# Router logits with tokens on partitions, and the full expert groups ahead of two rests

## The chip, the cores and the metric

The kernel runs on one core of a Trainium2 chip. The metric is device microseconds of one execution; lower is better. Before the change the median of three runs is 1096.84 us (1096.45 to 1098.13).

## What is computed

Three stages follow one another, all in float32.

```python
scores = where(causal, -1e9, q @ k.T / sqrt(D) + decay)      # 4 x 8 heads, 576 tokens, D = 64
x = softmax(scores) @ v                                       # reshaped to 2304 tokens x 512
h = x @ w_in;  x = (h * sigmoid(1.702 * h)) @ w_out           # 512 -> 2048 -> 512
noisy = x @ w_gate + log1p(exp(x @ w_noise)) * noise          # 8 experts
top2, weights = two largest of noisy, softmax over the two
out[t] += weight * (relu(x[t] @ w1[e]) @ w2[e])               # for each chosen expert e, 512 -> 1024 -> 512
```

## The kernel before

The program's order is made by a planner (class Planner) while it is built: the work is written as generators, each yields an engine, an estimated duration and a function that emits the instructions, and the planner picks by start time and priority. What it emits is then fixed: every engine, and the DMA queue on SP, works through its own list in order.

Products run on TensorE in pieces: each float32 operand is split into a rounded part (hi, type fp32r) and a remainder (lo), and a product is hi x hi, hi x lo and lo x hi. ScalarE makes hi, VectorE (sometimes POOL) makes lo.

Stages in time: attention by pairs of heads with the first quarter of the dense layer filling in (0 to some 240 us); the dense layer in chunks of 256 tokens and four quarters of its hidden dimension (to some 624 us); the experts (to the end). The last quarter of each chunk (step, line 1316) is followed by that chunk's routing (route, line 1165), nine times in all.

Routing of a chunk: the 256 rows of 512 values (pay) are transposed on TensorE, 4 matmuls for each half of 128 tokens (tr, line 1179), and split into yh and yl. The logits (line 1195) then have the gate weights as the stationary operand, and the tokens run past it:

```python
for kk in range(KD):
    nc.tensor.matmul(lg, wgs[:, kk], yh[:, kk], start=(kk == 0), stop=False)
    nc.tensor.matmul(lg, wgs[:, kk], yl[:, kk], start=False, stop=(kk == KD - 1))
```

Here wgs holds 32 columns, 16 rounded gate and noise weights and their 16 remainders, so lg is 32 partitions by 256 tokens. ScalarE copies it (line 1203), VectorE subtracts (1204), and two more matmuls with the selection matrix sel2 add the two halves and turn the result over (fold, line 1209), so that tokens lie on partitions; VectorE copies that into lz (1215). A chain of some 25 small VectorE instructions follows: noise, two largest, shares, and a place for each token in its expert's table. Four indirect DMAs on POOL (line 1286) scatter the rows into that table in HBM.

Experts: every expert has room for 640 table rows, five blocks of 128. A group (line 1395) is some blocks of one expert: it loads its rows, transposes and splits them, runs the first product (line 1539), relu and split (1522, 1523), the second product (1592), scales the rows and adds them into the output with an indirect DMA (1579). Groups run one after another in the order of the list:

```python
groups = [(e, 0, NBE) for e in EE] + [(e, NBE if e in EE else 0, NB) for e in range(E)]
```

With NEE = 2, NBE = 2 and NB = 5 that is: blocks 0 and 1 of experts 0 and 1 (the early groups, which start before all chunks are routed), then blocks 2 to 4 of experts 0 and 1, then all five blocks of experts 2 to 7. Each group fetches its expert's weights, 4 MB in pieces of 256 KB (wprep, line 357, loads on SP at line 374), however many blocks it has. The late groups wait until the last chunk's rows are scattered. Within a group all blocks are split before its first product is planned.

An expert below PEX (2) is called whole: its rows are loaded block by block (line 1426) and transposed by TensorE (1467). The others are loaded in strided pieces, eight loads and one small one for a group (1429, 1434), and transposed in 32x32 squares by VectorE (1473).

Of the kernel before, what the change touches and what calls it, by code (L numbers as in the profile page):

```python
# [8 lines left out]
F32 = mybir.dt.float32  # L9
FR = mybir.dt.float32r  # L10
# [4 lines left out]
OP = mybir.AluOpType  # L15
AX = mybir.AxisListType
# [1 line left out]
DRAM = bass.MemoryType.DRAM  # L18

TINY = 2.0 ** -15  # L20
PEX = 2
CAP = 640
EARLY = 256
NEE = 2
# [170 lines left out]
def act(n, sbuf=False, extra=0):  # L195
    return (n + (112 if sbuf else 61)) / 1200 + 0.093 * extra


def dve(n):
    return (n + 64) / 960  # L200
# [10 lines left out]
def mm(n, count=1):  # L211
    return count * max(0.109, 0.0024 + n * 0.0004506)
# [12 lines left out]
def tile_attn_mlp_moe(ctx, tc, q, k, v, f, w_in, w_out, gates, noise, w1, w2, out):  # L225
# [3 lines left out]
    nc = tc.nc  # L229
# [5 lines left out]
    E, FE = w2.shape[0], w2.shape[1]  # L235
    NP = B * H // 2
    PPB = H // 2
    KD = DM // 128
    CH = 256
# [27 lines left out]
    banks, dbanks = Tokens(range(2 * ND, 8)), Tokens(range(ND))  # L267
# [4 lines left out]
    def bank(i, name):  # L272
        return bplace[i].tile([128, 512], F32, name=name, tag=f"bank{i}")
# [4 lines left out]
    def c_(shape, name, dt=F32):  # L278
        return const.tile(shape, dt, name=name)

    identf = c_([128, 128], "identf")
# [10 lines left out]
    tokid = c_([128, NTL], "tokid")  # L292
    nzs = c_([128, NTL, E], "nzs")
    wgs = c_([128, KD, 32], "wgs", FR)
    sel2 = c_([64, 16], "sel2", FR)
    self_ = c_([64, 16], "self")
    cumc = c_([128, E], "cumc", BF)
    thr = c_([128, NOV], "thr")
    tiny = c_([1, 1], "tiny")
# [514 lines left out]
    def setup(one, init):  # L814
# [19 lines left out]
        def later():  # L834
            yield ("DMA", 0.1, lambda: nc.sync.dma_start(wgf, gates))
            yield ("DMA", 0.2, lambda: nc.sync.dma_start(nzs, noise))

            def rest():
                nc.vector.tensor_reduce(self_, identf[0:64, 0:64].rearrange("p (a c) -> p c a", c=16), axis=AX.X, op=OP.add)
                nc.vector.tensor_copy(sel2, self_)  # L840
                nc.vector.tensor_copy(wgs[:, :, 0:16], wgf)
                nc.vector.tensor_tensor(wgs[:, :, 16:32], wgf, wgs[:, :, 0:16].bitcast(F32), op=OP.subtract)
            yield ("DVE", 0.6, rest)

            def prest():
                nc.gpsimd.memset(cumc, 0.0)
                nc.gpsimd.memset(floor8, 0.0)
                nc.gpsimd.memset(floor8[:, 0:NEE], float(EARLY))
                nc.gpsimd.iota(iota8, pattern=[[1, E]], base=0, channel_multiplier=0, **io)
                nc.gpsimd.iota(ebase, pattern=[[RS, E]], base=0, channel_multiplier=0, **io)  # L850
                nc.gpsimd.iota(block, pattern=[[128, CAP // 128]], base=0, channel_multiplier=0, **io)
                nc.gpsimd.iota(thr, pattern=[[128, NOV]], base=CAP, channel_multiplier=0, **io)
                nc.gpsimd.iota(tokid, pattern=[[128, NTL]], base=0, channel_multiplier=1, **io)
                nc.gpsimd.memset(padr[:, 0:ROW - 1], 0.0)
                nc.gpsimd.iota(padr[:, ROW - 1:ROW], pattern=[[0, 1]], base=NT, channel_multiplier=1, **io)
            yield ("POOL", 1.5, prest)
            yield ("set", pad_ok)
# [234 lines left out]
    rt = lctx.enter_context(tc.tile_pool(name="route", bufs=2))  # L1092
# [13 lines left out]
    rest = [c for c in range(NCH) if c not in early_c]  # L1106
# [55 lines left out]
    def V(fn, us=0.08):  # L1162
        return ("DVE", us, fn)

    def route(pos, c, pay, evs, rti):
        tt, ts, stt = nc.vector.tensor_tensor, nc.vector.tensor_scalar, nc.vector.scalar_tensor_tensor
# [4 lines left out]
        a, b = yield from stages(2)  # L1171
        yh, yl = [stage(i, [128, KD, CH], FR, f"yt{x}") for i, x in ((a, "h"), (b, "l"))]
        ends = [event(), event()]
# [13 lines left out]
            yield ("set", ends[t])  # L1187
        for t in range(2):
            yield ("go", tr(t))
        for z in ends:  # L1190
            yield z
        bi = yield banks
        lg = bank(bi, "lg")[0:32, 0:CH]

        def logits():
            for kk in range(KD):
                nc.tensor.matmul(lg, wgs[:, kk], yh[:, kk], start=(kk == 0), stop=False)
                nc.tensor.matmul(lg, wgs[:, kk], yl[:, kk], start=False, stop=(kk == KD - 1))
        yield ("PE", mm(CH, 8), logits)
        yield (stok, a)  # L1200
        yield (stok, b)
        lgs = rt.tile([64, CH], FR, name="lgs", bufs=1)
        yield ("ACT", act(CH), lambda: nc.scalar.copy(lgs[0:32], lg))
        yield ("DVE", dve(CH), lambda: tt(lgs[32:64], lg, lgs[0:32].bitcast(F32), op=OP.subtract))
        yield (banks, bi)
        bi = yield banks
        l2 = bank(bi, "l2")[:, 0:32].rearrange("p (t e) -> p t e", t=2)

        def fold():
            for t in range(2):  # L1210
                nc.tensor.matmul(l2[:, t], lgs[:, t * 128:(t + 1) * 128], sel2, start=True, stop=True)
        yield ("PE", 0.2, fold)
        T = lambda n, sh, d=F32: rt.tile([128] + sh, d, name=n)
        lz = T("lz", [2, 16])
        yield V(lambda: nc.vector.tensor_copy(lz, l2), 0.1)
        yield (banks, bi)
        z = lz[:, :, E:2 * E]
        az, u, d, s2 = [T(n, [2, E]) for n in ("az", "u", "d", "s2")]
# [153 lines left out]
    NB = CAP // 128  # L1372
    NBE = EARLY // 128
    EE = list(range(NEE))
    groups = [(e, 0, NBE) for e in EE] + [(e, NBE if e in EE else 0, NB) for e in range(E)]
    W2 = {}
    for gi_, (e, b0, b1) in enumerate(groups):
        for j in range(FB):
# [372 lines left out]
```

## Time and profile before

| | us |
|---|---|
| median of 3 runs | 1096.84 |
| the profiled execution's own time | 1092.42 |
| its span, first to last instruction | 1090.6 |
| TensorE busy in the span | 1066.9 |

In the profile PE is TensorE's matmuls, PEld its weight loads (which overlap with them), DVE is VectorE, ACT ScalarE, POOL GpSimd, and SP the engine whose queue issues most DMAs. L1592 is line 1592 of the kernel. A merged line of the timeline has a count (x4), and its time goes from the first start to the last end. Matmuls are pipelined: one of 512 columns is shown with 0.39 us, but the next starts 0.23 us behind it, so distances between starts tell what a matmul costs. "<-" in brackets names what ended an engine's idle time.

### The profile page before, as it was taken

The numbers are of one execution on the slowest core, as the hardware profiler recorded it, in microseconds if no ns is written. First come the engines' busy times: TensorE is split into PE (matmuls) and PEld (weight loads), VectorE is DVE, ScalarE is ACT, GpSimd is POOL, SyncE is SP. The second block draws the span as 40 slices with busy tenths as digits, with TensorE's granted clock in tenths as the row PEclk, the third lists the DMA queues.
The fourth block names the chain that finished last, engine by engine and source line by source line (L and its number), as shares of the span: only waits on it lengthen the run. The fifth ranks groups of instructions, "written<-read, shape, count | busy, mean of one in ns | idle before, by whom it ended". The sixth has DMA issues, their size and how long they took to land.

```text
span 1090.6 us, 18989 instructions
## 1 busy us (share of the span) xinstructions
PE 1066.9 (98%) x6876; PEld 950.3 (87%) x6876; DVE 704.2 (65%) x1795; ACT 517.7 (47%) x1240; POOL 233.8 (21%) x274
## 2 busy tenths in 40 slices
PE   8999999999999999999999999999999999999996
PEld 7777788899999898999888887998999999999996
DVE  8889979866697468447888886576353535353321
ACT  7887888854554244224333444455342424242321
POOL 4246544200000000000234331132030303030302
PEclk9999999999999999999999999999999999999998
DMA  8888798657679903000122468988555554344413
GB/s 251 272 243 241 212 254 249 179 183 171 251 172 354 356 20 107 11 1 10 41 78 79 156 200 246 223 197 200 144 116 136 108 144 89 115 86 118 95 33 52
DMA packets 106552, 168.84 MB, mean 155 GB/s; under 512 B 15248, under 2 KB 47760, under 8 KB 106448
## 3 DMA queue, kind: packets, MB, share of 16 engines
q1 hardware_dynamic: 97808, 147.52, 46.0%
q0 software_dynamic: 8640, 20.00, 9.1%
q8 instruction: 56, 0.92, 0.4%
q14 instruction: 48, 0.39, 0.1%
HBM read 118.16 MB, written 49.32 MB: 154 GB/s over the span
## 4 chain that ended last, share of the span: by engine, by line
PE 83%; DVE 7%; DMA 3%; issue 3%; ACT 2%; POOL 1%; SPq 0%; POOLq 0%; DVEq 0%; ACTq 0%
PE h L1539 19%; PE ye L1592 19%; PE h L972 18%; PE y L992 17%; PE O L760 3%; PE PT L715 2%; PE S L626 2%; DVE e L601 1%; DMA rv<-in_v 1%; ACT e L607 1%; DMA rk<-in_k 1%; PE tr L1181 1%; DVE pt24l L473 1%; DMA out<-yt,eids 1%; DMA wraw<-in_w 1%
## 5 line engine op out<-in xcount | busy, mean ns | idle before, releaser
L1523 DVE SCALAR_TENSOR_TENSOR hl<-h,hh 128x256 fp32r<-128x256 f32 (+1 forms) x110 | 54.5, 499 | 172.4 <-ACT hh L1522 172.0
L1522 ACT ACTIVATE hh<-h 128x256 fp32r<-128x256 f32 (+1 forms) x110 | 48.9, 446 | 205.5 <-PE h L1539 205.4
L1579 POOL DMA_INDIRECT out<-yt,ids x36 | 61.8, 1717 | 296.9 <-ACT yt L1574 289.6
L992 PE MATMUL y<-wbh,gh 128*128 128x512 f32 x288 | 114.1, 396 | 0.0
L992 PE MATMUL y<-wbh,gl 128*128 128x512 f32 x288 | 112.6, 391 | 0.0
L992 PE MATMUL y<-wbl,gh 128*128 128x512 f32 x288 | 112.4, 390 | 0.0
L944 ACT ACTIVATE t<-h 128x256 f32<-128x256 f32 x144 | 55.2, 385 | 118.1 <-PE h L972 101.4
L1592 PE MATMUL ye<-wbh,hl 128*128 128x512 f32 x283 | 110.8, 392 | 0.0
L1592 PE MATMUL ye<-wbh,hh 128*128 128x512 f32 x283 | 110.7, 391 | 0.0
L1592 PE MATMUL ye<-wbl,hh 128*128 128x512 f32 x283 | 110.3, 390 | 0.0
L607 ACT ACTIVATE e<-e,m 128x128 f32<-128x128 f32 (+2 forms) x144 | 83.3, 581 | 24.7 <-DVE m L601 24.4
L1539 PE MATMUL h<-xtl,wah 128*128 128x256 f32 (+1 forms) x448 | 86.7, 312 | 0.0
L1539 PE MATMUL h<-xth,wah 128*128 128x256 f32 (+1 forms) x448 | 85.6, 312 | 0.0
L1539 PE MATMUL h<-xth,wal 128*128 128x256 f32 (+1 forms) x448 | 85.3, 312 | 0.0
L945 DVE SCALAR_TENSOR_TENSOR t<-t,h 128x256 f32<-128x256 f32 x144 | 59.9, 417 | 38.0 <-ACT t L944 35.2
L947 ACT CAST gh<-t 128x256 fp32r<-128x256 f32 x126 | 51.0, 406 | 56.1 <-DVE t L945 55.7
L1539 PEld LDWEIGHTS h<-xth,wah 128*128 128x128 f32 x448 | 74.3, 188 | 3.8 <-ACT wah L409 0.2
L354 DVE TENSOR_TENSOR gl<-t,gh 128x256 fp32r<-128x256 f32 x127 | 53.3, 422 | 29.6 <-ACT gh L947 28.3
L1539 PEld LDWEIGHTS h<-xtl,wah 128*128 128x128 f32 x448 | 71.5, 188 | 0.7
L1539 PEld LDWEIGHTS h<-xth,wal 128*128 128x128 f32 x448 | 71.3, 188 | 0.0
L354 DVE TENSOR_TENSOR wal<-wraw,wah 128x512 fp32r<-128x512 f32 x74 | 50.4, 687 | 27.3 <-ACT wah L409 26.8
L409 ACT CAST wah<-wraw 128x512 fp32r<-128x512 f32 x84 | 51.9, 623 | 28.9 <-DMA wraw<-in_w 28.7
(440 smaller groups left out, 2588.5 us busy)
## 6 DMA issues: line engine op xcount, KB each, us to landing
wraw<-in_w SPq DMA_DIRECT2D x160, 256.0 KB, 3.0
tab<-padr SPq DMA_DIRECT2D x40, 258.0 KB, 5.9
x<-xo SPq DMA_DIRECT2D x32, 288.0 KB, 2.3
bb<-cneg SPq DMA_DIRECT2D x15, 576.0 KB, 6.1
wraw<-in_w_in SPq DMA_DIRECT2D x16, 512.0 KB, 5.7
wraw<-in_w_out SPq DMA_DIRECT2D x16, 512.0 KB, 4.7
out<-padr SPq DMA_DIRECT2D x23, 256.0 KB, 5.2
xa<-x SPq DMA_DIRECT2D x22, 256.0 KB, 7.1
```

Source lines behind the costliest of these rows:

```text
L354: return ways(kind, ("DVE", dve(n), lambda: nc.vector.tensor_tensor(dst, a, b, op=OP.subtract), "port"), ("POOL", pool2(n), lambda: nc.gps ...
L409: yield ("ACT", act(n, True), lambda: nc.scalar.copy(hi, val))
L607: yield ("ACT", act(n, True, extra=2), lambda: nc.scalar.activation(dst, dst, AF.Exp, bias=m[:, x:x + 1], scale=-1.0, accum_out=sa[:, shar ...
L944: yield ("ACT", act(CH), lambda: nc.scalar.activation(t, h, AF.Tanh, scale=0.851))
L945: yield ("DVE", dve(CH), lambda: nc.vector.scalar_tensor_tensor(t, t, 1.0, h, op0=OP.add, op1=OP.mult))
L947: yield ways("gh", ("ACT", act(CH, True), lambda: nc.scalar.copy(gh, t)), ("POOL", pool1(CH), lambda: nc.gpsimd.tensor_tensor(gh, t, onec. ...
L972: nc.tensor.matmul(h, a[:, kk], z[:, kk], start=(i == 0), stop=(i == len(ops) - 1))
L992: nc.tensor.matmul(y, a[:, t * 128:(t + 1) * 128], b, start=(n_ == 0 and n == 0), stop=(n_ == FPQ - 1 and n == 2))
L1523: yield ("DVE", dve(c1 - c0), lambda: stt(hl[:, c0:c1], ps, 0.0, hh[:, c0:c1].bitcast(F32), op0=OP.max, op1=OP.subtract))
L1539: nc.tensor.matmul(ps, a[:, kk], z[:, kk, c0:c1], start=(i == 0), stop=(i == len(ops) - 1))
L1579: st = nc.gpsimd.indirect_dma_start(out=out, out_offset=bass.IndirectOffsetOnAxis(ap=ids[:, b:b + 1], axis=0), in_=yt, in_offset=None, com ...
L1592: nc.tensor.matmul(ye[b][0], a[:, b * 128:(b + 1) * 128], w, start=(j == 0 and n == 0), stop=(j == FB - 1 and n == 2))
```

## The change

Three things change. The transposed rows become the stationary operand of the logit matmuls and the 32 gate columns the moving one, separately for each half of 128 tokens, so that the logits come out with tokens on partitions; the copy, the subtraction and the fold go, the remainder's sixteen columns are copied and added by VectorE, and the selection matrix with its set-up is gone. The list of groups has experts 2 to 7 directly behind the early groups, and the rests of experts 0 and 1 at the end. PEX is 3, so expert 2 is whole too.

```diff
--- before.py
+++ after.py
@@ -18,7 +18,7 @@
 DRAM = bass.MemoryType.DRAM
 
 TINY = 2.0 ** -15
-PEX = 2
+PEX = 3
 CAP = 640
 EARLY = 256
 NEE = 2
@@ -292,8 +292,6 @@
     tokid = c_([128, NTL], "tokid")
     nzs = c_([128, NTL, E], "nzs")
     wgs = c_([128, KD, 32], "wgs", FR)
-    sel2 = c_([64, 16], "sel2", FR)
-    self_ = c_([64, 16], "self")
     cumc = c_([128, E], "cumc", BF)
     thr = c_([128, NOV], "thr")
     tiny = c_([1, 1], "tiny")
@@ -836,11 +834,9 @@
             yield ("DMA", 0.2, lambda: nc.sync.dma_start(nzs, noise))
 
             def rest():
-                nc.vector.tensor_reduce(self_, identf[0:64, 0:64].rearrange("p (a c) -> p c a", c=16), axis=AX.X, op=OP.add)
-                nc.vector.tensor_copy(sel2, self_)
                 nc.vector.tensor_copy(wgs[:, :, 0:16], wgf)
                 nc.vector.tensor_tensor(wgs[:, :, 16:32], wgf, wgs[:, :, 0:16].bitcast(F32), op=OP.subtract)
-            yield ("DVE", 0.6, rest)
+            yield ("DVE", 0.3, rest)
 
             def prest():
                 nc.gpsimd.memset(cumc, 0.0)
@@ -1187,32 +1183,23 @@
             yield ("set", ends[t])
         for t in range(2):
             yield ("go", tr(t))
-        for z in ends:
-            yield z
         bi = yield banks
-        lg = bank(bi, "lg")[0:32, 0:CH]
-
-        def logits():
+        lg = bank(bi, "lg")[:, 0:64].rearrange("p (t e) -> p t e", t=2)
+
+        def logits(t):
             for kk in range(KD):
-                nc.tensor.matmul(lg, wgs[:, kk], yh[:, kk], start=(kk == 0), stop=False)
-                nc.tensor.matmul(lg, wgs[:, kk], yl[:, kk], start=False, stop=(kk == KD - 1))
-        yield ("PE", mm(CH, 8), logits)
+                for x in (yh, yl):
+                    nc.tensor.matmul(lg[:, t], x[:, kk, t * 128:(t + 1) * 128], wgs[:, kk],
+                                     start=(kk == 0 and x is yh), stop=(kk == KD - 1 and x is yl))
+        for t in range(2):
+            yield ends[t]
+            yield ("PE", 0.056 * 2 * KD, lambda: logits(t))
         yield (stok, a)
         yield (stok, b)
-        lgs = rt.tile([64, CH], FR, name="lgs", bufs=1)
-        yield ("ACT", act(CH), lambda: nc.scalar.copy(lgs[0:32], lg))
-        yield ("DVE", dve(CH), lambda: tt(lgs[32:64], lg, lgs[0:32].bitcast(F32), op=OP.subtract))
-        yield (banks, bi)
-        bi = yield banks
-        l2 = bank(bi, "l2")[:, 0:32].rearrange("p (t e) -> p t e", t=2)
-
-        def fold():
-            for t in range(2):
-                nc.tensor.matmul(l2[:, t], lgs[:, t * 128:(t + 1) * 128], sel2, start=True, stop=True)
-        yield ("PE", 0.2, fold)
         T = lambda n, sh, d=F32: rt.tile([128] + sh, d, name=n)
-        lz = T("lz", [2, 16])
-        yield V(lambda: nc.vector.tensor_copy(lz, l2), 0.1)
+        lz, lo_ = T("lz", [2, 16]), T("llo", [2, 16])
+        yield V(lambda: nc.vector.tensor_copy(lo_, lg[:, :, 16:32]), 0.1)
+        yield V(lambda: tt(lz, lg[:, :, 0:16], lo_, op=OP.add), 0.1)
         yield (banks, bi)
         z = lz[:, :, E:2 * E]
         az, u, d, s2 = [T(n, [2, E]) for n in ("az", "u", "d", "s2")]
@@ -1372,7 +1359,7 @@
     NB = CAP // 128
     NBE = EARLY // 128
     EE = list(range(NEE))
-    groups = [(e, 0, NBE) for e in EE] + [(e, NBE if e in EE else 0, NB) for e in range(E)]
+    groups = [(e, 0, NBE) for e in EE] + [(e, 0, NB) for e in range(NEE, E)] + [(e, NBE, NB) for e in EE]
     W2 = {}
     for gi_, (e, b0, b1) in enumerate(groups):
         for j in range(FB):
```

## Rows read from the trace of the kernel before

**Rows 1.** The page, busy time and its share of the span
```profile
PE 1066.9 (98%) x6876; PEld 950.3 (87%) x6876; DVE 704.2 (65%) x1795; ACT 517.7 (47%) x1240; POOL 233.8 (21%) x274
```

**Rows 2.** Stages: us, busy PE, PEld, DVE, ACT, POOL; granted clock, DMA share, GB/s
```profile
0.00:240.00 240.00, 229.72 (x1783) 193.21 (x1783) 202.42 (x538) 189.69 (x533) 97.55 (x89) 1.00 0.79 231
...
500.00:624.00 124.00, 123.70 (x846) 111.22 (x845) 103.15 (x444) 44.72 (x113) 40.59 (x73) 1.00 0.22 78
624.00:682.00 58.00, 53.56 (x350) 45.63 (x348) 42.03 (x130) 30.30 (x63) 12.55 (x20) 1.00 0.72 215
682.00:748.00 66.00, 66.00 (x340) 60.07 (x339) 43.18 (x73) 31.65 (x60) 13.38 (x14) 1.00 0.88 214
```

**Rows 3.** TensorE's waits, 500 to 700 us: total, times, longest
```profile
PE h L1539 <- ACT wah L409: 0.9, 1, 0.9
...
PE po L1261 <- DVE hb L1254: 0.5, 2, 0.3
```

**Rows 4.** TensorE's timeline: start, us; a chunk's logits and a fold
```profile
616.69 0.40 PE L972 MATMUL h<-xl,wah 128*128 128x256 f32 x2
...
617.34 0.50 PE L972 MATMUL h<-xl,wah 128*128 128x256 f32 x2
...
632.54 0.28 PE L1197 MATMUL lg<-yth,wgs 128*32 128x256 f32 x1
...
633.48 0.39 PE L1592 MATMUL ye<-wbh,gh 128*128 128x512 f32 x1
```

**Rows 5.** Weight loads, timeline, then by line (ns min/median/max)
```profile
65.36 0.19 PEld L760 LDWEIGHTS O<-pt4h,vs 128*128 128x128 f32 x1
65.47 0.19 PEld L760 LDWEIGHTS O<-pt4l,vs 128*128 128x128 f32 x1
...
617.02 0.29 PEld L1211 LDWEIGHTS l<-sel,lgs 64*128 64x128 f32 x2
...
L1211 PEld LDWEIGHTS l<-sel,lgs x18: 182/184/186, 522.1 to 635.8; 64*128 64x128 f32 x18
...
L1197 PEld LDWEIGHTS lg<-yth,wgs x36: 107/108/112, 519.6 to 633.1; 128*32 128x32 f32 x36
```

**Rows 6.** One block's transposes: TensorE's timeline, then the chain that ended last
```profile
683.88 0.60 PE L1467 MATMUL tr<-identf,xe 128*128 128x128 f32 x4
684.24 0.94 PE L1539 MATMUL h<-xth,wah 128*128 128x384 f32 x4
...
684.04 0.44 PE tr L1467 x4
```

**Rows 7.** Between logits and lz: by line, then VectorE's timeline
```profile
L1203 ACT CAST lgs<-lg x9: 362/362/363, 520.8 to 633.7; 32x256 fp32r<-32x256 f32 x9
L1204 DVE TENSOR_TENSOR lgs<-lg,lgs x9: 412/414/415, 521.2 to 634.4; 32x256 fp32r<-32x256 f32 x9
...
637.03 0.18 DVE L1215 COPY lz<-l 128x32 f32<-128x32 f32 x1
```

**Rows 8.** The chain that ended last, around 664 us: start, us, what
```profile
657.73 6.28 DMA out<-yt,eids
```

**Rows 9.** Splits of late groups' blocks on VectorE, and TensorE's first late product
```profile
675.19 0.69 DVE L1477 TENSOR_TENSOR xtl<-tr,xth 128x512 fp32r<-128x512 f32 x1
...
685.72 0.68 DVE L1477 TENSOR_TENSOR xtl<-tr,xth 128x512 fp32r<-128x512 f32 x1
...
681.79 0.87 PE L1539 MATMUL h<-xth,wah 128*128 128x384 f32 x4
```

**Rows 10.** Busy time in one of the last microseconds, columns as in rows 2
```profile
1087.00:1088.00 1.00, 0.00 (x0) 0.00 (x0) 0.00 (x0) 0.00 (x0) 0.00 (x0) 0.50 0.35 66
```

**Rows 11.** VectorE's and POOL's timelines during the router's set-up
```profile
22.48 0.25 DVE L839 TENSOR_REDUCE self<-identf 64x16 f32<-64x64 f32 x1
22.76 1.65 DVE L840 CAST sel<-self 64x16 fp32r<-64x16 f32 x1
...
22.75 1.54 POOL L355 TENSOR_TENSOR ql<-rq,qh 128x640 fp32r<-128x640 f32 x1
```

## The prediction

> **What bounds the kernel now.** I read the shares of busy time first, then the stages, then the waits, then single instructions. TensorE is busy 98% of the span and no other engine passes 65% [rows 1]. By stages [rows 2]: attention (0 to 240 us) leaves TensorE 10.3 us idle, the routing stretch (500 to 624) 0.3, the stretch of the two early groups (624 to 682) 4.4, and from 682 to 748 it never stops, although the DMA engines are at 0.88. So work added to TensorE in the routing stretch or behind 682 adds to the time one for one, work taken off the other engines there is worth nothing, and a gain has to come out of attention or out of 624 to 682. TensorE's named waits there are small and of several kinds; the two that bear on the change are 0.9 us for a split weight and 0.5 for the router's one-hot sums [rows 3].
>
> **Logits, the old form.** One chunk's eight matmuls of 256 columns take 633.48 - 632.54 = 0.94 us from their first start to the next instruction [rows 4]. The fold: two h matmuls start at 616.69 and take 2 x 0.117 (0.94 / 8), so the next could start at 616.92; it starts at 617.34 [rows 4]. The fold costs 0.42. Together 1.36 us for each of nine chunks.
>
> **Logits, the new form.** Sixteen matmuls, each with a 128x128 stationary of its own and only 32 moving columns. No row has this form. The nearest are attention's 64-column matmuls, also fp32r with a 128x128 stationary, whose weight loads start 0.11 us apart (65.36, 65.47), and the two fold matmuls of 16 columns, whose merged loads take 0.29 against 0.184 for one, so 0.106 apart [rows 5]. With 16 and with 64 columns the step is the same, so the load of the 128 stationary columns sets the pace; a load of 32 columns lasts 108 ns against 190 [rows 5]. I take 0.11: 16 x 0.11 = 1.76, +0.40 a chunk, **+3.6 us** for nine. Lower bound: the four transposes of a block step by (684.24 - 683.88) / 4 = 0.09 [rows 6], so 1.44, +0.08 a chunk, +0.7. Upper bound: the fold lost about 0.2 beyond its two steps (0.42 - 0.22) on entry and exit; were that paid by each of the two runs of eight, 1.76 + 0.4 = 2.16, +0.80 a chunk, +7.2. I stay at 0.11 because those rows have the operand type and the stationary's shape. Eight of the nine chunks lie before 624, where nothing hides it.
>
> The Trainium skill, "TensorE: Matmul & The Clock Gate", section "Back-to-back issue gap", gives about 81 ns as the sustained spacing of load-and-matmul pairs at 128 columns; by that my estimate for sixteen would be 1.3 us and the logits would cost nothing more. The trace's pairs with fewer columns step by 106 to 110 ns [rows 5], and the measurement decides.
>
> **Beside TensorE** each chunk loses a ScalarE copy (0.36), a VectorE subtraction (0.41) and the copy of the logits (0.18) [rows 7], and gets a copy and an addition of 32 values, priced at 0.18 each: VectorE is 0.23 lighter a chunk, off the path. What shortens is the chain of a chunk's routing. In the last chunk the logit matmuls are issued by 633.48 [rows 4] and the logits copied at 637.03 [rows 7], 3.6 us; without copy, subtraction and fold about 1.0 remains, and the longer logits take 0.4, so it ends some 2.2 us earlier. Queued behind it stand the last chunk's scatters on POOL, the early outputs' scatter behind them, and on SP a weight load that waits for that scatter until 664.0 [rows 8], with the first load of a late group behind it. I credit what TensorE waits for on this chain, 0.9 + 0.5 = **-1.4 us** [rows 3]; bounds 0 and the 4.4 that the stretch is idle [rows 2].
>
> **PEX = 3.** Expert 2's five blocks are now loaded whole and transposed on TensorE: four matmuls a block, 0.36 from start to start, 0.44 in the chain with the entry [rows 6]. 5 x 0.44 = **+2.2 us**; bounds 0, if all fall into idle gaps, and 2.2. The five VectorE transposes that go were beside the path, worth 0. On SP eight strided loads and a small one become five loads: less issue, worth 0.
>
> **The new order.** Group sizes, and so matmul columns, stay the same; experts 0 and 1 still fetch their weights twice. Their rests (six blocks) take their TensorE transposes along to the end, and expert 2's blocks come in their place. The first late group's first matmuls now wait for five blocks, not three. Before, the third block's split ended at 675.88, and TensorE got there at 681.79 [rows 9]: 5.9 us of cover. The fifth block, then one of the next group and at its priority, was split at 686.40 [rows 9]. Now it has the first group's priority, and the chain ahead of it is 2.2 us shorter, so I cost this at 0; if it stayed where it was, the second half of the first product (12 x 0.117 = 1.4 us into the group) would wait 686.4 - 683.2 = 3.2 us. Expert 3's strided loads come earlier on SP, ahead of some weights; but the group then running has five blocks, so its weights last longer: 0.
>
> **The end.** The DMA engines finish the last scatters at about 1087.35 [rows 10]. The last block's path (product, scaling, scatter) is the same whether two or four blocks of its group went before it: 0.
>
> **Set-up.** The removed cast held VectorE for 1.65 us while POOL ran a subtraction of 1.54, and ended with it [rows 11]. The next cast, of the same kind, inherits that wait, so I take only the removed reduction's 0.25 [rows 11]: **-0.25 us**; bounds 0 and 1.9 (0.25 + 1.65).
>
> The Trainium skill, "SBUF — State Buffer", section "Who interferes with whom", says that VectorE casts and GpSimd share one port pair, and that the later one blocks fully. The 1.65 us beside POOL agrees [rows 11].
>
> **Sum:** 3.6 + 2.2 - 1.4 - 0.25 = +4.15 us. The profiled execution took 1092.42 us (span 1090.6 [rows 1] and 1.8 around it); it would take 1096.6. The runs' median is 1096.84, 4.4 above the profiled one. I add the sum to the median: **1101.0 us**.
>
> **Rivals.**
> (A) The new pairs step by 0.09, as the transposes do: 0.7 + 2.2 - 1.4 - 0.25 = +1.25, 1098.1: no difference that can be told. For it: the transposes have the same 128 stationary columns [rows 6]; against it: the 0.106 and 0.11 rows have the right type [rows 5].
> By the Trainium skill's 81 ns ("TensorE: Matmul & The Clock Gate", "Back-to-back issue gap") it would be 1096.8 as an estimate; rows 5 speak against it.
> (B) Faster: the supply of weights. Place: 624 to 748, DMA at 0.72 and 0.88 [rows 2], where four small groups in a row each ask for a full expert's weights. With only two in a row, the lead of the weights grows. Price: the 4.4 us idle before 682 and, if it sits in this supply, the 4.4 by which the median exceeds the profiled run: 3.6 + 2.2 - 8.8 - 0.25 = -3.25, 1093.6. It decides once more than 8 us come back. Against it: 682 to 748 has no idle time in the profile.
> (C) Late blocks: the fifth block comes when it came before, 3.2 us of stall and no credit: 3.6 + 2.2 + 3.2 - 0.25 = +8.75, 1105.6. For it: SP's order is in time, and weights have priority; against it: the 5.9 us of cover.
> (D) The change does not do what it says: the planner prices a new logit matmul at 0.056 us, half of what the rows show, and orders the queues by that, so routing ends later than planned and the credit is lost: +5.55, 1102.4. It lies within the forecast's own range.
>
> **Numbers.** Less than 0.2% (2.2 us) can't be told from no change. Forecast with D 0.42, A 0.22, B 0.26, C 0.10. Slower: forecast and C, 0.52; same: A, 0.22; faster: B, 0.26. The forecast alone spans 1098.6 (steps of 0.106, 3.0; transposes of 0.36, 1.8; credit 1.4; set-up 1.65: +1.75) to 1104.2 (no credit, and 0.2 of entry and exit once a chunk, 1.8: +7.35). The range has to reach B below and C above: 1093.0 to 1105.0 leaves out most of C and a part of B, some 2 in 10.
>
> **What would show it.** Right: sixteen logit matmuls a chunk at steps of about 0.11; the routing stretch some 3 us longer with TensorE still never idle; 44 transposes of late groups' rows; less than 4.4 us idle in the early groups' stretch. Wrong: logit steps of 0.09 or less (A); the early stretch shorter by more than its idle time (B); a gap in the first late group's first product (C).

## The result and the profile after

The changed kernel takes 1113.97 us (median of 4, 1112.14 to 1115.45) beside 1097.49 us for the kernel before in the same runs: a ratio of 1.0147 with an interval of 1.0112 to 1.0183, or 16.5 us slower. The forecast was 4 us slower, with a range up to 1105. The profiled execution took 1112.14 us, 19.7 more than that of before, which lay 5.1 under the median of its four runs here. One thing has to be known to read these numbers: repeated later, the same kernel was 12.2 us slower than before (1107.48 against 1095.32, ratio 1.0102, interval 1.0070 to 1.0134), and some 4 us of the first result did not come back (the two intervals overlap); they are taken apart below.

The busy shares of the page, then the stages, with the columns of [rows 2]:

```profile
PE 1084.1 (98%) x6950; PEld 961.8 (87%) x6950; DVE 699.9 (63%) x1797; ACT 513.6 (46%) x1236; POOL 222.5 (20%) x260
```

```profile
0.00:240.00 240.00, 229.31 (x1754) 191.79 (x1755) 200.52 (x532) 188.39 (x529) 96.20 (x88) 0.99 0.79 226
500.00:624.00 124.00, 123.40 (x867) 110.91 (x866) 97.07 (x429) 42.14 (x108) 31.53 (x60) 1.00 0.18 68
624.00:689.00 65.00, 61.79 (x403) 53.40 (x403) 48.52 (x159) 32.33 (x69) 14.20 (x22) 1.00 0.73 215
689.00:756.00 67.00, 67.00 (x377) 60.80 (x376) 39.47 (x71) 27.80 (x56) 15.48 (x17) 1.00 0.76 162
757.00:761.00 4.00, 2.04 (x12) 1.42 (x10) 0.00 (x0) 0.00 (x0) 0.00 (x0) 1.00 0.94 208
763.00:766.00 3.00, 3.00 (x8) 2.31 (x9) 0.90 (x2) 0.62 (x1) 0.00 (x0) 0.52 1.20 234
```

TensorE is busy 98% again, but 17 us longer [rows 1]. Two rows have no counterpart in [rows 2]: from 757 to 761 no engine but TensorE does anything and it is half idle, and from 763 to 766 its granted clock is 0.52, its lower level. The 0.99 of the first row is two stretches of 3.4 us at that level, from 22.4 and from 90.7 us. The profile of before has none there, but e17_before_again, the same kernel profiled later, has two as well (from 10.8 and from 89.3), so they are not the change's, though they are in the 19.7 us. The changed parts themselves look as they were priced. A chunk's sixteen logit matmuls, in TensorE's timeline (start, us), first, last and the next instruction:

```profile
577.66 0.18 PE L1192 MATMUL lg<-wgs,yth 128*128 128x32 f32 x1
...
579.25 0.26 PE L1192 MATMUL lg<-wgs,ytl 128*128 128x32 f32 x1
579.37 0.48 PE L968 MATMUL h<-xl,wah 128*128 128x256 f32 x2
```

They take 579.37 - 577.66 = 1.71 us, at steps of 0.11. In the set-up, the first cast that is left takes 0.38, and the instruction behind it 1.49, so the removed cast's wait beside POOL's subtraction was inherited (VectorE's timeline, then POOL's; [rows 11] for before):

```profile
22.51 0.38 DVE L837 CAST wgs<-wgf 128x64 fp32r<-128x64 f32 x1
22.93 1.49 DVE L838 TENSOR_TENSOR wgs<-wgf,wgs 128x64 fp32r<-128x64 f32 x1
...
22.80 1.53 POOL L353 TENSOR_TENSOR ql<-rq,qh 128x640 fp32r<-128x640 f32 x1
```

The surprise is what no line of the diff names. One hidden block of a five-block group (15 matmuls of the second product, then 24 of the first), in TensorE's timelines of before and of after: first matmul of the second product, first of the first product, and the second product's next start.

```profile
844.43 0.40 PE L1592 MATMUL ye<-wbh,hh 128*128 128x512 f32 x1
...
847.87 0.86 PE L1539 MATMUL h<-xth,wah 128*128 128x384 f32 x4
...
851.36 0.39 PE L1592 MATMUL ye<-wbh,hh 128*128 128x512 f32 x1
```

```profile
847.07 0.40 PE L1579 MATMUL ye<-wbh,hh 128*128 128x512 f32 x1
...
850.58 0.86 PE L1526 MATMUL h<-xth,wah 128*128 128x384 f32 x4
...
854.13 0.40 PE L1579 MATMUL ye<-wbh,hh 128*128 128x512 f32 x1
```

The same 39 instructions, with nothing to wait for and the clock at 1.00, take 6.93 us before and 7.06 after. Over 34 to 44 such periods of each trace, from 760 us on, the median is 6.92 us before and 7.02 after.

### The profile page after: what moved, and what is told of

It is laid out like the page before. It is cut to its first block, busy times and chain, and to the rows that moved or that the text cites. A ratio compares the mean times of both kernels' runs of the same rounds, so it can differ in the third digit from the quotient of the medians.

```text
span 1110.4 us, 19112 instructions
## 1 busy us (share of the span) xinstructions
PE 1084.1 (98%) x6950; PEld 961.8 (87%) x6950; DVE 699.9 (63%) x1797; ACT 513.6 (46%) x1236; POOL 222.5 (20%) x260
## 4 chain that ended last, share of the span: by engine, by line
PE 82%; DVE 6%; ACT 3%; DMA 3%; issue 2%; POOL 1%; SPq 0%; POOLq 0%; DVEq 0%; ACTq 0%
PE h L1526 18%; PE ye L1579 18%; PE h L968 18%; PE y L988 17%; PE O L758 3%; PE PT L713 2%; PE S L624 2%; DVE e L599 1%; PE lg L1192 1%; DMA wraw<-in_w 1%; ACT e L605 1%; DVE pt24l L471 1%; PE tr L1177 1%; POOL out L1566 1%; DMA xrh<-x 1%
## 5 line engine op out<-in xcount | busy, mean ns | idle before, releaser
L1579 PE MATMUL ye<-wbh,hh 128*128 128x512 f32 x285 | 113.2, 397 | 3.1 <-ACT hh L1509 3.1
L1579 PE MATMUL ye<-wbl,hh 128*128 128x512 f32 x285 | 113.4, 398 | 0.0
L1579 PE MATMUL ye<-wbh,hl 128*128 128x512 f32 x285 | 113.2, 397 | 0.1
L352 DVE TENSOR_TENSOR gl<-t,gh 128x256 fp32r<-128x256 f32 x134 | 56.2, 422 | 26.6 <-ACT gh L943 25.0
L988 PEld LDWEIGHTS y<-wbh,gl 128*128 128x128 f32 x288 | 54.0, 188 | 13.9 <-DVE gl L352 2.0
L1579 PEld LDWEIGHTS ye<-wbh,hh 128*128 128x128 f32 x285 | 53.7, 189 | 14.2 <-ACT hh L1509 3.5
```

The costliest lines, as they stand in the source:

```text
L352: return ways(kind, ("DVE", dve(n), lambda: nc.vector.tensor_tensor(dst, a, b, op=OP.subtract), "port"), ("POOL", pool2(n), lambda: nc.gps ...
L988: nc.tensor.matmul(y, a[:, t * 128:(t + 1) * 128], b, start=(n_ == 0 and n == 0), stop=(n_ == FPQ - 1 and n == 2))
L1579: nc.tensor.matmul(ye[b][0], a[:, b * 128:(b + 1) * 128], w, start=(j == 0 and n == 0), stop=(j == FB - 1 and n == 2))
```

## Experiments

The built programs tell why the steps could differ. The tiles of the expert stage are laid out one behind the other in the order in which they are first asked for, at multiples of 32 bytes. With the new order the first late group has five blocks and, being transposed on TensorE, no separate tile for its routing columns; its small tile wab has 40 bytes instead of 24, so everything behind it moves by 32 bytes. The x tiles went from a multiple of 128 bytes to 32 beyond one, and the h tiles moved too. I started with that, and with the three parts of the change one at a time. "Period" below is the median time from one hidden block of a five-block group to the next.

**Shift alone, both ways.** The changed kernel with its shift partly undone, and the kernel before with nothing but a shift:

```diff
-            wab = M["x"].tile([128, 2, nb], F32, name="wab", tag=f"wab{gi_}")
+            wab = M["x"].tile([128, 2 * nb + (8 if gi_ == len(EE) else 0)], F32, name="wab", tag=f"wab{gi_}")
+            wab = wab[:, 0:2 * nb].rearrange("p (a b) -> p a b", a=2)
```

> The changed kernel, its order of instructions untouched, with one tile of the experts' pool 32 bytes longer, so that the split rows (xth, xtl) and the hidden values (hh, hl) begin at multiples of 64 bytes again, as they did before the change, instead of 32 beyond one. Theory 1 (addresses): the experts' second-product matmuls go back from 0.2337 to 0.2285 us from start to start and the 384-column ones from 0.1745 to 0.1729; some 960 times 0.0052 and 768 times 0.0016 make 6 us, so 16.5 us slower than before becomes about 10. Theory 2 (the longer step comes from the order of the groups or from the chip, not from addresses): the steps stay at 0.2337 and the time stays 16 us above before. Either way the 3 us stall of TensorE near 759 us stays.

> The kernel before with the same 32 bytes added, which here moves the same tiles off the multiples of 64. Theory 1 (addresses): steps of 0.2337 and 0.1745 and 6 us more than before (ratio about 1.0055), with the order of all instructions as before. Theory 2: no change.

Measured: e1_after_pad 1103.02 us beside 1095.15, ratio 1.0071 (1.0048 to 1.0095), period 6.97. e2_before_pad, the kernel before with one tile 32 bytes longer, 1102.29, ratio 1.0074 (1.0047 to 1.0101), period 7.04, and its instructions in unchanged order. Addresses alone cost 7 us.

**Logits alone, order alone.** e3_logits is the changed kernel with PEX = 2 and the old list of groups; e4_order_pad is the kernel before with PEX = 3, the new list and the 32 bytes of e1_after_pad. First against after, then against before:

```diff
-PEX = 3
+PEX = 2
-    groups = [(e, 0, NBE) for e in EE] + [(e, 0, NB) for e in range(NEE, E)] + [(e, NBE, NB) for e in EE]
+    groups = [(e, 0, NBE) for e in EE] + [(e, NBE if e in EE else 0, NB) for e in range(E)]
```

```diff
-PEX = 2
+PEX = 3
-    groups = [(e, 0, NBE) for e in EE] + [(e, NBE if e in EE else 0, NB) for e in range(E)]
+    groups = [(e, 0, NBE) for e in EE] + [(e, 0, NB) for e in range(NEE, E)] + [(e, NBE, NB) for e in EE]
```

> The change without its second and third part: the new logits alone, PEX 2 and the old order of groups; the tiles stay at multiples of 64. By the prediction's terms nine times 0.4 on TensorE less what the shorter routing gives back: +2 to +4 us (ratio 1.002 to 1.004). If the logits are what went wrong, 10 us or more. If attention's lost clock (two stretches at half speed, 3.6 us) comes with the shorter set-up and not by chance, it shows here as well and the sum is +6 to +8.

> The second and third part alone, with the old logits: PEX 3 and the new order, and the 32 bytes, so that addresses don't count. Theory: 2.2 us for expert 2's transposes on TensorE and, if the stall at the first late group's end comes with the order (a weight split queued on POOL behind five scatters, the weight loads behind it on SP), 5 us for the stall and the clock lost after it: +5 to +8 (ratio 1.005 to 1.007). Rival: the stall hangs on the shifted routing and is not in the order itself: +2.

Measured: e3_logits 1097.08, ratio 1.0019 (0.9998 to 1.0039), period 6.92. The stretch from 624 to 682 lost less than before (58 - 55.85 = 2.2 us idle, not 4.4 [rows 2]):

```profile
500.00:624.00 124.00, 124.00 (x889) 114.11 (x888) 100.65 (x448) 44.82 (x113) 32.55 (x61) 1.00 0.22 78
624.00:682.00 58.00, 55.85 (x369) 49.05 (x368) 43.02 (x141) 29.14 (x62) 12.63 (x20) 1.00 0.77 229
```

TensorE's waits from 500 to 700 us differ as follows. Before has these two beside the two of [rows 3]; e3_logits shows none of the four, and one that before has only with 0.3 us, for a block's rows:

```profile
PE h L1539 <- DVE cumc L1268: 0.7, 1, 0.7
PE h L1539 <- DVE xrl L1477: 0.7, 1, 0.7
```

```profile
PE tr L1454 <- DMA xe<-tab: 1.7, 1, 1.7
```

e4_order_pad 1101.57, ratio 1.0060 (1.0043 to 1.0078), period 6.97, with no stall near 755. So the 5 to 8 us that were expected of it came (6.4), but without the stall that was to make most of them: luck.

**The phase as before.** Two pads bring the first x tiles and the h tiles of the changed kernel to the addresses of before, and the other x tiles to a multiple of 128 bytes: 24 more values in that wab, 32 in the last group's. e5_after_phase:

```diff
+            pad_ = {2: 24, len(groups) - 1: 32}.get(gi_, 0)
-            wab = M["x"].tile([128, 2, nb], F32, name="wab", tag=f"wab{gi_}")
+            wab = M["x"].tile([128, 2 * nb + pad_], F32, name="wab", tag=f"wab{gi_}")
+            wab = wab[:, 0:2 * nb].rearrange("p (a b) -> p a b", a=2)
```

e7_order_phase has the same pads on e4_order_pad in place of its own, and e8_order_pex2 is the kernel before with the new list of groups and nothing else.

> The changed kernel with its x and h tiles of the expert stage put back to the kernel before's phase (x tiles at a multiple of 128 bytes, h tiles 64 beyond one); instructions and their order as in the changed kernel. Theory (the phase of the operand addresses sets the matmul step, in three levels): the period per hidden block of a five-block group falls from the 6.97 us of e1_after_pad to 6.92 us, as in the kernel before; 48 such periods and 16 of three blocks give about 2.9 us, so some 1100 us (e1_after_pad: 1103.0). The stall of 3 to 4 us at 755 stays. Rival (the phase gave all it had at 64 bytes; the order of the groups or the third expert's transposes lengthen the step): the period stays at 6.97 us and the time at 1103 us.

> The kernel before with the new order of groups and the third expert's transposes on TensorE, logits as before, and the tiles at the kernel before's phase. Theory (phase): the period falls from the 6.97 us of e4_order_pad to 6.92 us and the time by 2.9 us from 1101.6 to 1098.7 us; what stays above the kernel before is the transposes, 5 x 0.44 = 2.2 us, and small waits in the early stretch. Rival: 6.97 us and 1101.6 us.

> The kernel before with the new order of groups alone: two experts' transposes on TensorE as before, logits as before; the tiles come to the kernel before's phase by themselves. Theory: the period is 6.92 us, no stall at 755, and the time is that of the kernel before within 1.5 us, 2.2 us below e7_order_phase. Rival (VectorE's transposes of the first late group come too late once it is a five-block group, which is why the change moves them): a wait of 1 to 4 us at the start of that group near 682, and a time at or above that of e7_order_phase.

Measured: e5_after_phase 1112.85 beside 1098.40, ratio 1.0141 (1.0112 to 1.0169), period 7.00; e7_order_phase 1104.70, ratio 1.0062 (1.0038 to 1.0086), period 7.00. My theory fell: with the addresses of before the period rose. e8_order_pex2 1105.04, ratio 1.0056 (1.0037 to 1.0075), though with a period of 6.93: there the rival came true. VectorE's timeline, late in the first late group's supply:

```profile
695.39 0.75 DVE L1572 TENSOR_SCALAR yt<-ye,ewab 128x512 f32<-128x512 f32 x1 [3.90 <-DMA out<-yt,eids]
696.06 0.70 DVE L1473 STREAM_TRANSPOSE xf<-xe 128x512 f32<-128x512 f32 x1
696.68 0.65 DVE L1477 TENSOR_TENSOR xtl<-xf,xth 128x512 fp32r<-128x512 f32 x1
```

A VectorE scaling waits 3.9 us for an output scatter, the transpose of a late block stands behind it, and TensorE's waits have 2.7 us that end with that scaling. This is what the third expert's transposes on TensorE avoid; the order alone would not have done.

**Distance, not phase.** What tells e5_after_phase from before is that in the changed kernel the weight tiles lie 128 bytes lower (two constants are gone) while its h tiles were put exactly where before has them. So I sorted the runs by the distance of the h tiles from the w2 tiles. In the second product h is the stationary operand and w2 the moving one. All later runs are in the table too:

| kernels | h minus w2, remainder of 256 bytes | x tiles, remainder of 128 | period |
|---|---|---|---|
| before, e3_logits | 0 | 0 | 6.92 |
| e14_before_h256 | 0 (256 more than before) | 0 | 6.92 |
| e13_before_dve, e17_before_again | 0 | 0 | 6.92 |
| e8_order_pex2, e9_after_h, e11_h_dve, e15_order_dve, e18_h_again | 0 | 0 | 6.93 |
| e10_h_only | 0 | 32 | 6.95 |
| e1_after_pad, e4_order_pad | 192 | 64 | 6.97 |
| e5_after_phase, e6_phase_dve, e7_order_phase, e12_yt_back | 128 | 0 | 7.00 |
| after, e16_after_again | 160 | 32 | 7.02 |
| e2_before_pad | 32 | 32 | 7.04 |

e9_after_h is e5_after_phase without its second pad (96 bytes in all, distance 0). e10_h_only puts them behind the x tiles. e14_before_h256 is the kernel before with h 256 bytes on. The pads of the three:

```diff
+            pad_ = {2: 24, len(groups) - 1: 0}.get(gi_, 0)
+            pad_ = {2: 0, len(groups) - 1: 24}.get(gi_, 0)
+            pad_ = {2: 0, len(groups) - 1: 64}.get(gi_, 0)
```

e12_yt_back is e5_after_phase with a tile ahead of the outputs 384 bytes longer, because the output tiles had moved with h in every run:

```diff
-        over = M["y"].tile([128, E, NOV], F32, name="over")
+        over = M["y"].tile([128, E * NOV + 96], F32, name="over")[:, 0:E * NOV].rearrange("p (e o) -> p e o", e=E)
```

> The changed kernel with one tile 96 bytes longer, so that the h tiles lie at the same remainder of 512 bytes as the weight tiles that they are multiplied with. The runs so far, by the distance of the h tiles from the w2 tiles (remainder of 512): 0 gave a period of 6.92 to 6.93 us, 64 short of it 6.97 us, 128 beyond it 7.00 us, 32 beyond or 96 short 7.02 to 7.04 us. New theory (the distance between the stationary h tile and the moving weight tile sets the step, neither address by itself): period 6.92 us, and 48 x 0.08 + 16 x 0.05 = 4.6 us below e5_after_phase, so 10 us above the kernel before; the stall at 755 stays. Rival (the third expert's transposes on TensorE, common to all that were long but one): the period stays at 6.97 us or more.

> As e9_after_h, but the 96 bytes lie behind the x tiles, which stay where the changed kernel has them (32 bytes beyond a multiple of 64). If the distance of h from the weights is all, the period is 6.92 us as in e9_after_h; if the x tiles' place counts too, it is between 6.94 and 7.02 us and the steps of the first product (128x384 and 128x256) are the longer ones.

> e5_after_phase (h tiles 128 beyond the weights' remainder, period 7.00 us) with the output tiles, which had moved together with the h tiles in all runs, put back to the remainder that they have in e9_after_h. If the h tiles decide: period 7.00 us. If it is the output tiles (written by ScalarE and VectorE while TensorE reads): 6.92 us.

> The kernel before with its h tiles 256 bytes further, nothing else. Theory as it stands: the distance of h from the w2 tiles counts; 0 gave 6.92 us, 64 either way about 6.97 us, 128 gave 7.00 us. If it counts by remainders of 256 bytes, the period stays 6.92 us; by remainders of 512, it is 7.00 us or more. If the distance were not what counts, no change: 6.92 us too, so only a longer period tells against the first reading.

Measured: e9_after_h 1099.87 beside 1095.31, ratio 1.0043 (1.0025 to 1.0061), period 6.93. e10_h_only 1098.26 in one run, 6.95 (mean 6.94, against 6.93). e12_yt_back 1102.79 in one run, 7.00: not the output tiles. e14_before_h256 1096.69 in one run, 6.92: remainders of 256. TensorE's timeline in three kernels, five periods apart: e1_after_pad (34.86 us), e5_after_phase (35.05) and e9_after_h (34.65).

```profile
842.08 0.64 PE L1527 MATMUL h<-xth,wal 128*128 128x256 f32 x4
...
876.94 0.64 PE L1527 MATMUL h<-xth,wal 128*128 128x256 f32 x4
```

```profile
848.07 0.64 PE L1528 MATMUL h<-xth,wal 128*128 128x256 f32 x4
...
883.12 0.63 PE L1528 MATMUL h<-xth,wal 128*128 128x256 f32 x4
```

```profile
844.09 0.64 PE L1528 MATMUL h<-xth,wal 128*128 128x256 f32 x4
...
878.74 0.63 PE L1528 MATMUL h<-xth,wal 128*128 128x256 f32 x4
```

**The stall at 759.** In after, TensorE waits 3.1 us there for ScalarE's h. The chain, by the timelines of POOL, of SP's queue and of ScalarE:

```profile
745.47 1.57 POOL L1566 DMA_INDIRECT out<-yt,ids  x1 [38.84 <-ACT hh L1509]
...
753.17 1.91 POOL L1566 DMA_INDIRECT out<-yt,ids  x1 [0.27 <-issue]
754.51 1.89 POOL L353 TENSOR_TENSOR wal<-wraw,wah 128x512 fp32r<-128x512 f32 x1
```

```profile
745.15 11.61 SPq L372 DMA_DIRECT2D wraw<-in_w  x2
756.85 1.89 SPq L1416 DMA_DIRECT2D xe<-tab  x4
```

```profile
761.07 0.62 ACT L407 CAST wah<-wraw 128x512 fp32r<-128x512 f32 x1 [9.45 <-DMA wraw<-in_w]
761.59 0.76 ACT L1509 ACTIVATE hh<-h 128x384 fp32r<-128x384 f32 x2
```

The planner gave a weight's remainder (wal) to POOL, where it stands behind the five output scatters of the first late group (745.47 to 753.17). The weight's slot comes free only then, so SP holds its queue from 745.15 to 756.76, with 10.4 us put down to POOL's spacer, a small write on the far side of that split. The waits of SP's queue and of TensorE from 700 to 800 us (total, times, longest):

```profile
SPq L372 <- POOL spacer L1565: 10.7, 2, 10.4
```

```profile
PE ye L1579 <- ACT hh L1509: 3.1, 1, 3.1
```

The load lands, ScalarE casts at 761.07, and the h of the running product, behind that cast in ScalarE's order, follows at 761.59. After the pause TensorE runs at the low clock, and the second product's steps are 0.43 us instead of 0.23:

```profile
764.65 0.63 PE L1579 MATMUL ye<-wbh,hh 128*128 128x512 f32 x1
765.08 0.63 PE L1579 MATMUL ye<-wbl,hh 128*128 128x512 f32 x1
```

e6_phase_dve, e11_h_dve, e13_before_dve and e15_order_dve keep POOL out of it, with one line behind the routing stage: on e5_after_phase, on e9_after_h, on the kernel before, and on the new order with the old logits and distance 0.

```diff
     P.run(m1_done)
+    WAYS['wl'] = ('DVE',)
```

> e5_after_phase, with the weights' low parts of the expert stage split on VectorE alone, so that none is queued on GpSimd behind the output scatters. Theory (a split behind five scatters holds the weight ring, then the weight load on SP, then ScalarE's cast and the eviction behind it): no wait on hh above 1 us between 740 and 780, no stretch at clock 0.5 after it; 3.1 to 3.6 us of idle and 2 us at half clock go, so 5 us below e5_after_phase, some 1095 us. Rival (the transfers of that time are what is late, x loads, scatters and weights together): the wait moves by under 1.5 us and the time by under 2 us. A third way: VectorE, with 13 more splits, becomes late itself, and the time rises.

> e9_after_h with the weights' low parts of the expert stage split on VectorE alone (as in e6_phase_dve): the changed kernel with both repairs. Theory: period 6.92 us, no stall at 755; 4.6 us below e6_phase_dve, so 1.0022 times the kernel before: what is left is the logits' 1.9 us (e3_logits) and the third expert's transposes, 5 x 0.44 = 2.2 us, less small gains. Rival (the distance is not it): 1.0064 times as e6_phase_dve.

> The kernel before with nothing changed but the weights' low parts of the expert stage split on VectorE alone. If GpSimd's splits behind the scatters cost the kernel before nothing (it shows no stall near 755), the time is that of the kernel before, ratio 1.000 within 0.002. If the 2 us that e11_h_dve lies under the sum of its parts come from there, 0.998 to 0.999, and this version beats both kernels. A loss would show VectorE late with its 7 more splits.

> The kernel before with the new order of groups, the third expert's transposes on TensorE, the h tiles at the weights' remainder and VectorE's splits: e11_h_dve without the new logits and the set-up. Theory: period 6.92 us, no stall; 2 us (e3_logits: 1.0019) below e11_h_dve's 1.0015, so 1.000 within 0.002: the order and the transposes alone give back what they cost. Rival (the order and the transposes, 5 x 0.44 us, stand for the whole of e11_h_dve's rest and the logits for nothing next to them): 1.0015 to 1.002.

Measured: e6_phase_dve 1104.19 against e5_after_phase's 1112.85, 8.7 us less where 5 were expected; no wait on hh is left. e11_h_dve 1096.84 beside 1095.31, ratio 1.0015 (0.9999 to 1.0031), 3.0 us below e9_after_h. The medians thus put the stall at 8.7 and at 3.0 us; in the profiled executions the time from the first late product to the last instruction is 419 us in e5_after_phase against 414 in e6_phase_dve, and 416 in e9_after_h against 410 in e11_h_dve, some 5 us each. e13_before_dve 1097.20 beside 1097.79, ratio 0.9993 (0.9971 to 1.0015): worth nothing in the kernel before. e15_order_dve 1100.56, ratio 1.0009 (0.9988 to 1.0030): it can't be told from e11_h_dve, so what is left is not split between the logits and the transposes. From 748 to 772, e9_after_h and then e11_h_dve:

```profile
748.00:772.00 24.00, 20.58 (x106) 17.86 (x106) 7.76 (x15) 6.21 (x13) 0.24 (x2) 0.93 0.77 162
```

```profile
748.00:772.00 24.00, 24.00 (x133) 21.50 (x132) 10.96 (x24) 6.74 (x14) 3.69 (x4) 1.00 0.81 181
```

**The rest of the 16 us.** After, e5_after_phase and e6_phase_dve share something that e9_after_h to e12_yt_back, with the same instructions in the same order as e5_after_phase (e11_h_dve apart from its splits), do not have: in the routing stretch TensorE waits for the dense layer's g. e7_order_phase, e8_order_pex2 and e13_before_dve to e15_order_dve, all with the old logits, have the unexplained idle time too. TensorE's waits of e5_after_phase from 500 to 640 us, then VectorE's unexplained ones there ("issue": idle for nothing that the profile shows):

```profile
PE y L988 <- ACT gh L943: 2.4, 7, 0.6
```

```profile
DVE t L941 <- issue: 2.3, 2, 1.8
```

From the first chunk's logits to the last chunk's it is 119.8 us in e5_after_phase, 117.6 in after, 113.5 in e9_after_h; with the old logits and the old order it is 116.2 in e14_before_h256 and 112.9 in before. The changed kernel, the kernel before and e9_after_h once more, on one chip:

> The changed kernel itself, once more. The runs so far fall into two kinds. In one (the kernel before, e1 to e4, e9 to e12) ScalarE and VectorE never idle without a reason that the trace shows between 500 and 640 us, and with the new logits the pitch of the chunks is 14.0 us. In the other (the changed kernel, e5 to e7, e13 to e15) they idle 1 to 5 us there for nothing that the trace shows, TensorE waits 0.3 to 0.6 us a chunk on ScalarE's g, and with the new logits the pitch is 14.4 to 15 us; the kernels of one call are all of one kind. Theory (the chip on which a kernel runs brings this, and the new logits suffer more from it than the old): if this call is of the first kind, 11 us above the kernel before (e1_after_pad's 7.9 and 2.9 of the period), pitch 14.0; if of the second, 16 us and 14.4 or more. Rival (it belongs to the changed kernel and its tiles' places): pitch 14.4 to 15 and 16 us whatever the others of this call show.

> The kernel before itself, for a trace from the same chip as the other two of this call. First kind of chip: no unexplained idle time of ScalarE and VectorE between 500 and 640 us, last chunk's logits 18.0 us after the one before. Second kind: 1 us or more of it, and 19.6 to 21 us there, as in e13 to e15. If the changed kernel is of the second kind here and this one of the first, the chip is not what tells them apart.

> e9_after_h once more, beside the changed kernel: the same instructions on the same chip, the h tiles 96 bytes further. Theory: 5 to 6 us below e16_after_again (48 periods of five blocks at 0.09 to 0.10 us, 16 of three at 0.05) on either kind of chip, its pitch of chunks equal to that of e16_after_again, period 6.93 us. Rival (the place of the h tiles also sets the routing stretch): pitch 14.0 us where e16_after_again has 14.4 or more, and 10 us below it.

Measured: e16_after_again 1107.48 beside 1095.32 (ratio 1.0102), its nine chunks' logits span 113.5 us, no unexplained idle time, period 7.02. e17_before_again 1093.03, 112.9 us, period 6.92. e18_h_again 1100.51, ratio 1.0042 (1.0025 to 1.0060), 113.5 us, period 6.93. So the waits do not belong to the changed kernel or to its tiles' places. The chip was the one of e5_after_phase, so neither are they a property of that chip: of the kernels that ran together at one time, every trace has them or none has. What they are, the traces don't show.

## Why the prediction was wrong

The sign was right; the size was off by a factor of three to four. By its steps:

- **Logits: right in their price.** 1.71 us a chunk against 1.76 forecast and 1.36 before. By themselves the logits with the lighter routing and the set-up were put at 3.6 - 1.4 - 0.25 = +1.95 us; e3_logits measured 1.0019, 2 us (-0.2 to 4.3 by its interval). So rival A's step of 0.09 did not come: at 128x128 stationary and 32 columns this kernel's pairs step by 0.11. Nor did the 81 ns that the Trainium skill ("TensorE: Matmul & The Clock Gate", "Back-to-back issue gap") states.
- **The credit of 1.4 us: met in size, in part by luck.** The idle time of the early groups' stretch fell by 2.2 us, but the credit was taken from two waits, and two others (cumc and xrl, 0.7 each) went as well, while one of 1.7 for a block's rows came; the credited 0.9 for a split weight is also missing from e17_before_again, where nothing was changed. The sign "the routing stretch some 3 us longer" did not come: from the first chunk's logits to the last chunk's it is 112.9 us before and 113.5 in e3_logits; TensorE's idle time in it, which fell from 1.7 to 0.1 us, makes most of the difference.
- **Set-up:** the removed cast's wait was inherited, though by the subtraction behind the next cast and not by that cast. The 0.25 us was not measured alone.
- **Transposes and the last groups' end:** not measured alone. e11_h_dve, both parts with both repairs, lies 1.5 us above before (-0.1 to 3.4). The 4.15 that was forecast for the same parts lies above that, so a term of the sum was too high or something came back that the sum does not have; the runs don't tell which.
- **The new order, cost 0: wrong**, and this is the step that failed. "Group sizes, and so matmul columns, stay the same" is true, but I took from it that each matmul costs the same. The list of groups also sets the order in which tiles are laid out. The h tiles came to 160 bytes from the w2 tiles by remainders of 256, and the period grew from 6.92 to 7.02. Six groups of five blocks have 48 such periods (8 hidden blocks each): 4.8 us, and the 16 of three blocks about 1 more. e16_after_again stands 7.0 us above e18_h_again; in their traces its pause at the stall is longer too (2.9 us against 2.5), and the clock falls behind it, which it does not in e18_h_again, so not all of the 7.0 need be the distance.
- **A stall behind the first late group: not foreseen.** I looked for a late block at that group's start (rival C) and named its five-block length only as more time for weights. But five blocks also mean five output scatters in a row on POOL, 9 us from the first one's start to that of the weight split behind them (745.47 to 754.51). Pause and low clock together cost 3.0 us by the medians of e9_after_h and e11_h_dve (each has an interval of some 2 us to either side) and some 5 in their traces. Part of it is luck of the planner: in e4_order_pad, with the same list of groups, the split behind the scatters is one of the second product's weights (wbl), and TensorE does not stop.
- **Some 4 us of the first result** belong, as far as the traces tell, to the time of the runs and not to the change: 16.5 us then, 12.2 in the repeat, and the nine chunks' logits span 117.6 us then, 113.5 in the repeat.

7.0 for the distance, 3.0 for the stall and 1.5 for the rest are 11.5 of the repeat's 12.2 us; each of them is known to some 2 to 4 us, so this shows that no large part is missing, and not how the 12.2 divide to the microsecond. Rival B (weights sooner) found nothing to give back: from 689 to 756 TensorE was never idle, as from 682 to 748 before [rows 2]. Rival D is not needed: with the logits priced as they were, the credit came.

No version beat the kernel before. The change with both repairs, e11_h_dve, equals it within its interval.

## What to carry to other kernels

A change to the order of work is also a change to the memory map. When the same instructions step slower with nothing to wait for and the clock full, compare tile addresses before looking for a mechanism in the schedule; here a pad of 32 bytes on the old kernel, with nothing else changed, made it 7 us longer. And when a group grows, count what it will put in a row on the engine that issues the scatters, and what stands behind them.

## What was not expected of the hardware

- In these runs the step of the second product's matmuls went with where their two operands lie to each other. With 128x128 stationary h and 512 moving columns of w2, fifteen steps took 3.42 to 3.44 us at distance 0, 3.45 at 192, 3.49 at 128, 3.50 in after (160) and 3.52 in e2_before_pad at 32 (means over 24 to 31 periods each). The Trainium skill, "SBUF — State Buffer", section "Who interferes with whom", gives TensorE a read port for the moving operand and one for the weight load and calls them independent. The fifteen steps differ by 2% where only the distance differs (e5_after_phase against e9_after_h). That it is those two reads that meet is an inference: the w2 tiles moved together with all tiles laid out before them.
- The first product doesn't read h, and its time goes with the other column of the table: 3.50 to 3.51 us where the x tiles lie at a multiple of 128 bytes, at distances 0 and 128 alike, and 3.52 to 3.54 where they don't. e10_h_only differs from e9_after_h in the x tiles' place alone and has 3.52 against 3.51. Of the period's 0.10 us between e9_after_h and after, some 0.08 are the second product's and 0.015 the first's.
- After a pause of 3.1 us TensorE's clock fell to its lower level (0.52 granted from 763 to 766) and the steps went from 0.23 to 0.43 us; in e11_h_dve, without the pause, it stayed at 1.00. In e18_h_again it stayed at 1.00 after a pause of 2.5 us:

```profile
757.02 0.50 PE L1581 MATMUL ye<-wbh,hh 128*128 128x512 f32 x1 [2.47 <-ACT hh L1511]
```

```profile
757.00:763.00 6.00, 5.91 (x33) 5.16 (x34) 2.42 (x6) 1.86 (x4) 0.00 (x0) 1.00 1.17 231
```

- ScalarE and VectorE together idled 2.4 to 6.0 us in the routing stretch for nothing that the profile shows, in every trace taken at one time and in none taken at another, on the same chip.
